# Warm-up products in column strips, and three weight loads in another place, in a fused state-space and feed-forward kernel

## The chip, the core and the metric

The kernel runs on one core of one Trainium2 chip. The metric is the device time of one execution in microseconds (us). A core has five engines with a queue of instructions each: TensorE (PE in the profile, its weight loads PEld), VectorE (DVE), ScalarE (ACT), GpSimd (POOL) and SyncE (SP). They wait for one another through semaphores. Transfers are started by SP, ACT or POOL and are carried out by 16 DMA engines. TensorE writes into PSUM, eight banks of 128 x 512 numbers in float32, which ACT or DVE has to read out before a bank can be used again.

## The reference

`x` is 2048 tokens by 512 features. After a layer norm, `xn`, two branches are computed from it and added to `x`:

```
xn  = layernorm(x)
# branch A, a diagonal complex state-space layer
Bu  = xn @ B_bar.T                       # complex, 512 states
h_t = Lam_bar * h_(t-1) + Bu_t           # along 2048 tokens
yA  = 2 * real(h @ C.T) + xn * Dskip
# branch B, a gated feed-forward layer with 1376 hidden units
yB  = (silu(xn @ w_gate) * (xn @ w_up)) @ w_down
out = x + yA + yB
```

Products take bfloat16 and accumulate in float32; the output is bfloat16.

## The kernel before

The 2048 tokens are cut into four chunks `c` of 512 tokens (four tiles of 128 tokens each). Each chunk goes through the same products on TensorE, all of them written out by hand in one order:

- `bproj_tile(c, part, q)` (L365): B's product, real (`part` 0) and imaginary (`part` 1), for four groups `q` of 128 states. It sums four products over the feature blocks `k` into one PSUM bank, with `BT[:, part, k]` as the weights, and ACT copies the bank to `u16` (L372).
- `gateup_tile(c, fi)` (L511): for each of ten full blocks `fi` of 128 hidden units a gate bank and an up bank, each of four products (L445); ACT applies silu to the one and copies the other (L464, L465), DVE multiplies them in pairs of blocks (L460). The eleventh block has only 96 units. For it `gateup_last(c)` (L500) computes the 96 gate columns together with 32 of the up columns (`w_last`), read out by L506 and L507. The other 64 up columns (`wu_last`) are computed for all four chunks at once in `up_halves` (L484, products in L492, in pairs of 64 columns), much later, within `out_chunk(0)`.
- `out_ffn`, `out_pair` and `out_ssm`: the products with `w_down` and with C.

DVE turns the complex recurrence into real scans (rotations L380 to L394, scans L412). Its work is kept in a list, `backlog`, and `pump` puts pieces of it behind each TensorE tile by costs written in the code, so the order on every engine is fixed when the program is built.

The head (L686 to L726) handles the first chunk. While the first tokens are on their way, TensorE runs dummy products on a constant (`dummy(8, CW)`, eight products of 512 columns, then two of 128, L687 and L688; the product is in L660). Then it transposes the first token tiles by products with an identity (L235), and computes gate and up columns of three blocks tile by tile (`head_mm`, L683). The normalisation is on DVE (L220). The last tile of the chunk, and all tiles of later chunks, are transposed by a transfer instead (`xT_dma`, L249, on SP).

Weights are loaded in groups of hidden blocks, `fgroups` (L89): blocks 0 to 1, 2, 3 to 6 and 7 to 9. Most transfers stand on SP's queue in the order of the code: at the start x's first tiles, the first three weight groups and two of B's transposed loads; then `load_mid()` (L143) with x's second chunk, B's remaining real transposes, its four imaginary transposes (`load_bt(1, k)`, L138), the last gate group, the last up group and `w_last`; then the transposes of chunk 1's tokens; then `load_late()` (L154) with x's second half and `w_down` in two halves (L159); then C's eight transposes (L862). `load_late` also puts the load of `wu_last` on ACT's queue (L155). It is called after chunk 0's B products and ahead of its blocks 7 to 10:

```
    load_late()
    for fi in range(G0, FT):
        gateup_tile(0, fi)
```

after which come C's transposes and `bproj_chunk(1)` (L789, called in L864). An engine's queue is in order: a transfer that ACT starts stands among ACT's copies, and if its issue has to wait, what is behind it waits too. Each transfer that SP or ACT starts uses one of eight completion counters, chosen when the program is built.

Of the kernel before, what the change touches and what calls it, by code (L numbers as in the profile page):

```python
# [23 lines left out]
def kernel(  # L24
# [17 lines left out]
    nc = tc.nc  # L42
    _, L, D = A_x.shape
# [3 lines left out]
    CW = 512  # L47
# [4 lines left out]
    KD = D // 128  # L52
    HK = KD // 2
# [6 lines left out]
    LA, LB = 32, 64  # L60
    FL = (FT - 1) * 128
# [12 lines left out]
    def bank(shape=(128, CW), dtype=F32):  # L74
        return psum.tile(list(shape), dtype, name="ps")
# [6 lines left out]
    wg_v = B_w_gate.rearrange("(k p) f -> p k f", p=128)  # L82
    wu_v = B_w_up.rearrange("(k p) f -> p k f", p=128)
# [6 lines left out]
    wg_g, wu_g = [], []  # L90
# [5 lines left out]
    wu_last = const.tile([128, KD, LB], BF16, name="wu_last")  # L96
# [14 lines left out]
    def load_w1(q, tiles, view, gi):  # L111
        a, b = fgroups[gi]
        q.dma_start(out=tiles[gi][:], in_=view[:, :, a * 128:min(F, b * 128)])
# [23 lines left out]
    def load_bt(part, k):  # L137
        nc.sync.dma_start_transpose(out=BT[:, part, k, :], in_=(A_B_re, A_B_im)[part][:, k * 128:(k + 1) * 128])  # L138
# [4 lines left out]
    def load_mid():  # L143
        nc.sync.dma_start(out=xall[:, TPC:2 * TPC, :], in_=x_v[:, TPC:2 * TPC, :])
        for k in range(HK, KD):
            load_bt(0, k)
        for k in range(KD):
            load_bt(1, k)
        load_w1(nc.sync, wg_g, wg_v, 3)
        load_w1(nc.sync, wu_g, wu_v, 3)  # L150
        nc.sync.dma_start(out=w_last[:, :, 0:LB + LA], in_=wg_v[:, :, FL:F])
        nc.sync.dma_start(out=w_last[:, :, LB + LA:128], in_=wu_v[:, :, FL + LB:F])

    def load_late():  # L154
        nc.scalar.dma_start(out=wu_last[:], in_=wu_v[:, :, FL:FL + LB])  # L155
        nc.sync.dma_start(out=xall[:, 2 * TPC:NT, :], in_=x_v[:, 2 * TPC:NT, :])
        wd_v = B_w_down[0:FL, :].rearrange("(k p) d -> p k d", p=128)
        for a, b in ((0, FT // 2), (FT // 2, FT - 1)):
            nc.sync.dma_start(out=wd_sb[:, a:b, :], in_=wd_v[:, a:b, :])  # L159


    ones = nc.const_aps.tensor(1.0, (128, CW), BF16)
# [348 lines left out]
    def gateup_tile(c, fi):  # L511
        if fi == FT - 1:
            return gateup_last(c)
        psg = bank()
        gu_mm(psg, wg_g, c, fi, 0, CW)
        psu = bank()
        gu_mm(psu, wu_g, c, fi, 0, CW)
        gu_out(c, fi, psg, psu)
# [113 lines left out]
    def pump(us):  # L632

        owed[0] += us
        while backlog and owed[0] >= backlog[0][0] * 0.5:
            step()
        if not backlog:
            owed[0] = 0.0

    def multiply(keep):  # L640

        while len(products) > keep:
            products.pop(0)()
            owed[0] -= 0.65
# [10 lines left out]
    held = [(bank(), bank()) for _ in range(H)]  # L655
    warm = held[0][0]

    def dummy(n, cols):
        for _ in range(n):
            nc.tensor.matmul(warm[:, 0:cols], lhsT=ones[:, 0:128], rhs=ones[:, 0:cols], start=True, stop=True)  # L660
# [23 lines left out]
                                 rhs=xnT[:, k, lo * 128:hi * 128], start=(k == 0), stop=(k == KD - 1))  # L684

    allk = range(KD)  # L686
    dummy(8, CW)  # L687
    dummy(2, 128)  # L688
    ln_stats(0)
    rstd_act(0)  # L690
# [4 lines left out]
    rstd_act(1)  # L695
    xT_pe(0, on_dve=(0,))
    dummy(4, 128)
    norm_dve(1)
    ln_stats(2)
# [20 lines left out]
    norm_dve(3)  # L720
    xT_dma(3)
    load_mid()
    head_mm(0, 2, 3, range(0, HK), range(H))
    head_mm(1, 2, 3, range(0, HK), range(H))
# [55 lines left out]
    for fis in (range(4, EARLY - 1), range(EARLY - 1, EARLY)):  # L780
        ps, n = bank(), len(fis)
# [59 lines left out]
    for part in range(2):  # L841
        for q in range(NQ):
# [10 lines left out]
           ["ln2"] * len(norm2) + ["ln3"] * (len(stats3) + len(norm3)))  # L853
    queue("cf", c_ops())
    load_late()
    for fi in range(G0, FT):
        gateup_tile(0, fi)
        pump(GU)
        multiply(1)
    for part, src in enumerate((A_C_re, A_C_im)):  # L860
        for q in range(NQ):
            nc.sync.dma_start_transpose(out=CT[:, part, q, :], in_=src[:, q * 128:(q + 1) * 128])  # L862
# [50 lines left out]
```

## Time and profile before

| | |
|---|---|
| median of 3 runs | 178.35 us |
| lowest and highest | 178.32 and 178.7 us |
| profiled execution | 178.76 us |
| its span, first to last instruction | 177.0 us |
| TensorE busy | 173.5 us, 98% of the span |
| DVE busy | 153.9 us, 87% |
| ACT busy | 95.3 us, 54% |
| POOL busy | 51.8 us, 29% |
| moved by DMA | 16.36 MB, mean 92 GB/s |

The profile is of one execution. A row of a timeline gives start and length in us from the span's start, then the engine, the line of the kernel, the operation, what it writes and reads, its shape, how many such instructions are merged in the row, and in brackets the idle time ahead of it with what ended it. "SPq" and "ACTq" are the issues of transfers from those queues; a row of the DMA view gives the size and the time from issue to landing. The length of a TensorE product in a row includes its way through the array, so products overlap, and the distance between starts is what a product costs. TensorE's clock is half at the beginning of a run and again some time after the last product.

### The profile page before, as it was taken

Reading aid. Unit: us, or ns where it says so; the run is one execution under the profiler, and the core shown is the slowest. Engines: PE = TensorE matmul, PEld = TensorE weight load, DVE = VectorE, ACT = ScalarE, POOL = GpSimd, SP = SyncE. Lnnn points to the kernel's source line nnn. Section 1 sums busy time; section 2 is a strip of 40 time slices with the busy share of each in tenths; the row PEclk is TensorE's granted clock in tenths of the full one; section 3 lists DMA queues with packets and bytes.
Section 4 is the critical chain, followed back from the end, with each engine's and each line's share of the span. In section 5 each row is a group of like instructions: output and inputs, shape, how many; then the busy total and the mean of one; then the engine's idle time right before and its main releaser. Section 6 shows DMA issues by size and latency. Waiting matters only on the chain.

```text
span 177.0 us, 2607 instructions
## 1 busy us (share of the span) xinstructions
PE 173.5 (98%) x955; PEld 84.1 (48%) x955; DVE 153.9 (87%) x233; ACT 95.3 (54%) x174; POOL 51.8 (29%) x86
## 2 busy tenths in 40 slices
PE   8999999999999999999999999999999999999993
PEld 2977644444444444444444444444444444444443
DVE  3779999999999997999999999999999999971033
ACT  3477898867797679613666661053866610001300
POOL 6050120002300210029997040058476500001410
PEclk9999999999999999999999999999999999999999
DMA  5998497996440014900000020019699200000652
GB/s 169 306 167 204 91 257 80 305 305 129 89 87 6 0 36 82 355 5 17 17 19 17 0 82 11 0 20 129 88 147 189 46 2 0 0 4 0 63 98 76
DMA packets 31292, 16.36 MB, mean 92 GB/s; under 512 B 20208, under 2 KB 31088, under 8 KB 31248
## 3 DMA queue, kind: packets, MB, share of 16 engines
q1 hardware_dynamic: 24704, 11.51, 27.3%
q0 software_dynamic: 5184, 4.07, 15.9%
q10 hardware_dynamic: 1392, 0.62, 1.7%
q8 instruction: 7, 0.11, 0.3%
q14 instruction: 5, 0.04, 0.1%
HBM read 8.33 MB, written 5.24 MB: 77 GB/s over the span
## 4 chain that ended last, share of the span: by engine, by line
PE 98%; DVE 0%; issue 0%
PE ps L445 35%; PE ps L594 16%; PE ps L370 16%; PE ps L556 10%; PE ps L582 10%; PE ps L683 2%; PE ps L660 2%; PE ps L503 2%; PE ps L759 2%; PE ps L545 2%; PE ps L492 1%; PE ps L235 1%; DVE res L599 0%; PE ps L265 0%
## 5 line engine op out<-in xcount | busy, mean ns | idle before, releaser
L445 PE MATMUL ps<-xnT,wg 128*128 128x512 bf16 (+1 forms) x148 | 36.6, 373 | 0.0
L445 PE MATMUL ps<-xnT,wu 128*128 128x512 bf16 (+1 forms) x148 | 36.6, 373 | 0.0
L412 DVE TENSOR_TENSOR_SCAN g<-r_t,car,u 128x512 bf16<-128x512 f32 x24 | 28.8, 1263 | 0.0
L370 PE MATMUL ps<-xnT,BT 128*128 128x512 bf16 x128 | 28.3, 379 | 0.0
L594 PE MATMUL ps<-CF,wt 128*128 128x512 bf16 (+2 forms) x144 | 28.2, 356 | 0.0
L464 ACT ACTIVATE guT<-ps 128x512 bf16<-128x512 f32 (+1 forms) x40 | 23.5, 587 | 6.7 <-PE ps L445 6.0
L465 ACT CAST u<-ps 128x512 bf16<-128x512 f32 (+1 forms) x40 | 23.0, 575 | 6.9 <-PE ps L445 6.6
L607 ACT CAST res<-ps 128x512 bf16<-128x512 f32 x12 | 6.7, 590 | 36.0 <-PE ps L594 26.8
L445 PEld LDWEIGHTS <-wu 128*128 128x128 bf16 x148 | 14.5, 98 | 16.6
L187 POOL DMA_DIRECT2D gu_rows<-ul x36 | 17.6, 499 | 15.8 <-DVE ul L480 15.8
L445 PEld LDWEIGHTS <-wg 128*128 128x128 bf16 x148 | 14.4, 98 | 16.5
L608 POOL DMA_DIRECT2D out_dram<-res x12 | 10.5, 1220 | 37.4 <-ACT res L607 37.2
L372 ACT CAST u<-ps 128x512 bf16<-128x512 f32 x32 | 18.2, 586 | 6.0 <-PE ps L370 5.9
L594 PEld LDWEIGHTS <-wt 128*128 128x128 bf16 x144 | 13.3, 98 | 15.0 <-issue 1.3
L370 PEld LDWEIGHTS <-BT 128*128 128x128 bf16 x128 | 12.5, 98 | 14.8
L212 POOL TENSOR_TENSOR rstd<-ve,neg_half 128x2 f32<-128x2 f32 (+1 forms) x4 | 5.7, 1418 | 44.4 <-DVE ve L211 44.4
L582 PE MATMUL ps<-wd_sb,guT 128*128 128x512 bf16 x80 | 17.6, 379 | 0.0
L556 PE MATMUL ps<-wd_sb,guT 128*128 128x512 bf16 x80 | 17.4, 379 | 0.0
L460 DVE TENSOR_TENSOR guT<-guT,u 128x1024 bf16<-128x1024 bf16 x20 | 13.4, 677 | 0.0
L582 PEld LDWEIGHTS <-guT 128*128 128x128 bf16 x80 | 7.8, 98 | 9.4
L556 PEld LDWEIGHTS <-guT 128*128 128x128 bf16 x80 | 7.8, 98 | 9.4
L203 DVE BATCH_NORM_STATS2 stats<-xall 128x6 f32<-128x512 bf16 x14 | 9.5, 679 | 1.9 <-DMA xall<-in_A_x_dram 1.8
(120 smaller groups left out, 200.8 us busy)
## 6 DMA issues: line engine op xcount, KB each, us to landing
out_dram<-in_A_x_dram SPq DMA_DIRECT2D x1, 1536.0 KB, 6.8
out_dram<-res POOLq DMA_DIRECT2D x12, 128.0 KB, 3.6
out_dram<-xall POOLq DMA_DIRECT2D x3, 512.0 KB, 7.4
wd_sb<-in_B_w_down_dram SPq DMA_DIRECT2D x2, 640.0 KB, 7.7
xall<-in_A_x_dram SPq DMA_DIRECT2D x1, 1024.0 KB, 5.9
gu_rows<-ul POOLq DMA_DIRECT2D x36, 8.0 KB, 1.6
wg<-in_B_w_gate_dram SPq DMA_DIRECT2D x1, 512.0 KB, 5.0
wu<-in_B_w_up_dram SPq DMA_DIRECT2D x1, 512.0 KB, 6.0
```

What stands on the lines that cost most here:

```text
L187: nc.gpsimd.dma_start(out=gu_rows[c][i * RT:(i + 1) * RT, p, :], in_=product[p * RT:(p + 1) * RT, i * 128:(i + 1) * 128])
L370: nc.tensor.matmul(ps[:], lhsT=BT[:, part, k, q * 128:(q + 1) * 128], rhs=xnT[:, k, c * CW:(c + 1) * CW], start=(k == 0), stop=(k == KD - 1))
L372: nc.scalar.copy(out=u_tiles[c][:, part, q, :], in_=ps[:])
L412: V.tensor_tensor_scan(out=g()[:, part, q, :], data0=r_t[:, q:q + 1].to_broadcast([128, CW]), data1=u_tiles[c][:, part, q, :], initial=ini ...
L445: nc.tensor.matmul(ps[:fs, lo:hi], lhsT=wslice(groups, fi, k), rhs=xnT[:, k, c * CW + lo:c * CW + hi], start=(k == 0), stop=(k == KD - 1))
L460: products.append(lambda: V.tensor_tensor(out=g, in0=g, in1=u, op=ALU.mult))
L464: nc.scalar.activation(out=gu_tile(c)[:, fi, 0:hi], in_=psg[:, 0:hi], func=ACT.Silu)
L465: nc.scalar.copy(out=u_tile(c, fi)[:, fi % 2, 0:hi], in_=psu[:, 0:hi])
L556: nc.tensor.matmul(o[:], lhsT=gu_tiles[k][:, fi, i * 128:(i + 1) * 128], rhs=wd_sb[:, fi, :], start=(fi == 0), stop=False)
L582: nc.tensor.matmul(o[:], lhsT=gu_tiles[c][:, fi, i * 128:(i + 1) * 128], rhs=wd_sb[:, fi, lo:hi], start=(fi == 0), stop=False)
L594: nc.tensor.matmul(o, lhsT=w_tiles[c][:, part, q, i * 128:(i + 1) * 128], rhs=CF[:, part, q, lo:hi], start=(fresh and part == 0 and q == 0 ...
L608: nc.gpsimd.dma_start(out=out_v[:, n, :], in_=res[:], accum_op=ALU.add)
```

## The change

Three edits. The first two of the eight 512-column dummy products become eight products with 32 weight columns each, four per set, written to the four 32-partition strips of the same bank. In `load_mid` the last gate group is loaded between B's second and third imaginary transpose, and the last up group behind the fourth; the number of transfers is the same. The load of `wu_last` stays on ACT's queue but moves from `load_late` to behind chunk 0's last gate and up block, which is behind that block's copy L507 and ahead of the copies L372 of `bproj_chunk(1)`.

```diff
-        for k in range(KD):
-            load_bt(1, k)
-        load_w1(nc.sync, wg_g, wg_v, 3)
-        load_w1(nc.sync, wu_g, wu_v, 3)
+        for groups, view, ks in ((wg_g, wg_v, range(0, HK)), (wu_g, wu_v, range(HK, KD))):
+            for k in ks:
+                load_bt(1, k)
+            load_w1(nc.sync, groups, view, 3)
...
     def load_late():
-        nc.scalar.dma_start(out=wu_last[:], in_=wu_v[:, :, FL:FL + LB])
         nc.sync.dma_start(out=xall[:, 2 * TPC:NT, :], in_=x_v[:, 2 * TPC:NT, :])
...
+    def dummy_groups(n):
+        for _ in range(n):
+            for i in range(0, 128, 32):
+                nc.tensor.matmul(warm[i:i + 32], lhsT=ones[:, 0:32], rhs=ones[:], start=True, stop=True)
+
...
-    dummy(8, CW)
+    dummy_groups(2)
+    dummy(6, CW)
     dummy(2, 128)
...
         multiply(1)
+    nc.scalar.dma_start(out=wu_last[:], in_=wu_v[:, :, FL:FL + LB])
     for part, src in enumerate((A_C_re, A_C_im)):
```

## The prediction

> **What bounds the kernel now.** I read the page's busy times and its chain first, then busy time by stretches, then the timelines around each edit. In the rows by stretches the columns are the length, then busy time of PE, weight loads, DVE, ACT and POOL, the granted clock, the DMA share and GB/s.
>
> ```profile
> span 177.0 us, 2607 instructions
> PE 173.5 (98%) x955; PEld 84.1 (48%) x955; DVE 153.9 (87%) x233; ACT 95.3 (54%) x174; POOL 51.8 (29%) x86
> PE 98%; DVE 0%; issue 0%
> ...
> 6.68:38.71 32.03, 32.03 (x245) 19.03 (x242) 29.05 (x70) 26.42 (x55) 4.17 (x5) 1.00 0.95 210
> 31.96 6.91 PE ps L370 x32
> ```
>
> The chain that ended last is TensorE for 98% of the span, and between 6.68 and 38.71 us TensorE has no gap at all. So nothing that only relieves another engine can shorten the run, and any wait put in front of TensorE lengthens it by its full length: there is no slack later in which to make it up. A full product of 512 columns costs 6.91/32 = 0.216 us, a product tile of four 0.864 us. What is left to win lies ahead of 6.68 us, where products take twice as long per column:
>
> ```profile
> 0.78 3.78 PE L660 MATMUL ps<-const-bfloat16-1.0 128*128 128x512 bf16 x10 [0.78 <-PEq L897]
> 4.11 0.41 DVE L220 TENSOR_SCALAR xall<-xall,mv,rstd 128x512 bf16<-128x512 bf16 x1
> 4.25 0.31 PE L660 MATMUL ps<-const-bfloat16-1.0 128*128 128x128 bf16 x1
> 4.58 0.61 PE L235 MATMUL ps<-ident,xall 128*128 128x128 bf16 x4
> 5.37 0.41 DVE L220 TENSOR_SCALAR xall<-xall,mv,rstd 128x512 bf16<-128x512 bf16 x1
> 6.26 0.59 PE L235 MATMUL ps<-ident,xall 128*128 128x128 bf16 x4
> 6.68 0.61 PE L683 MATMUL ps<-xnT,wu 128*128 128x128 bf16 x8
> 7.14 0.38 PE L683 MATMUL ps<-xnT,wg 128*128 128x128 bf16 x4
> ```
>
> The 4352 dummy columns take 3.78 us (0.87 ns each); eight products of 128 columns from 6.68 to 7.14 take 0.46 us (0.45 ns each), those from 6.26 to 6.68 take 0.42 us for four (0.82 ns). The clock turns up at about 6.68 us. The sum below is made against the profiled execution, 178.76 us (span 177.0 plus 1.76 around it); the median of the runs is 178.35, 0.41 lower, so the same difference is laid on the median.
>
> **Part 1, the dummies.** Two products over the full array become eight of 32 columns in four column strips. Nothing in the trace runs four strips; the nearest rows are the pairs of half-width products of L492:
>
> ```profile
> 71.73 0.81 PE L582 MATMUL ps<-wd_sb,guT 128*128 128x512 bf16 x3
> 72.47 1.92 PE L492 MATMUL ps<-xnT,wu_last 128*64 128x512 bf16 x16
> 74.32 0.39 PE L594 MATMUL ps<-CF,wt 128*128 128x512 bf16 x1
> ```
>
> Sixteen half-width products take 1.85 us up to the next full one, against 8 x 0.216 = 1.73: the two strips of a pair run side by side, with 0.12 for leaving the mode; three full products take 0.74 instead of 0.65 ahead of them, 0.09 for entering it. So two sets of four should take about as long as two full products, plus some 0.2 us for leaving at half clock. The dummies' products stop issuing at about 4.36 (the last starts at 4.25 and takes 0.11 at this clock) and the transposes of 4.58 wait for the normalisation that ends at 4.52, so 0.2 of it is covered. Bounds: 0 (they cannot make the transposes start before 4.52) and, if strips ran one after another, 6 x 0.43 = 2.6 us more dummies less the cover, of which about half, 1.2 us, would be left because the rest would then run after the clock has turned. The L492 rows are near the lower end: I take 0.05 us.
>
> **Part 2, SP's order.** The last gate group's load moves ahead of B's last two imaginary transposes.
>
> ```profile
> 18.85 7.07 PE L370 MATMUL ps<-xnT,BT 128*128 128x512 bf16 x32
> 18.62 1.26 SPq L138 DMA_TRANSPOSE BT<-in_A_B_im_dram  x1
> 19.93 0.58 SPq L113 DMA_DIRECT2D wg<-in_B_w_gate_dram  x1
> ...
> BT<-in_A_B_im_dram SPq DMA_TRANSPOSE x1, 2.7
> ```
>
> The last transpose now lands at 18.62 + 2.7 = 21.3. TensorE needs it for the fourth product of the first imaginary tile: B's products start at 18.85 (16 real ones at 0.216, then three more), so at 22.95: 1.6 us of cover. The load ahead of it costs its issue, 0.58, and its transfer, bounded by nothing and about 1.3 us (384 KB at the 300 GB/s of the row 30.70:39.20 below); 0.6 to 1.9 us later, so a wait of 0 to 0.3 us. I take 0; what there is would be swallowed by part 3, whose end does not depend on it. The gate group lands earlier, but TensorE does not wait for it now: gain 0.
>
> **Part 3, the last up columns.** The load of wu_last leaves ACT's queue at 25.97 and comes back behind the last copy of chunk 0's gate and up work (L507). Taking it out is a gain for the transfers:
>
> ```profile
> 23.14 1.22 SPq L249 DMA_TRANSPOSE xnT<-xall  x1
> 25.76 2.48 SPq L249 DMA_TRANSPOSE xnT<-xall  x1
> 28.32 1.29 SPq L249 DMA_TRANSPOSE xnT<-xall  x1
> 30.91 0.68 SPq L159 DMA_DIRECT2D wd_sb<-in_B_w_down_dram  x1
> 25.97 0.41 ACTq L155 DMA_DIRECT2D wu_last<-in_B_w_up_dram  x1
> wd_sb<-in_B_w_down_dram SPq DMA_DIRECT2D x1, 640.0 KB, 8.3
> ...
> 30.70:39.20 8.50, 8.50 (x41) 3.88 (x40) 8.36 (x15) 6.79 (x13) 0.00 (x0) 1.00 1.05 300
> ```
>
> The one slow transpose issue (2.48 against 1.2 to 1.3) is the one beside wu_last's transfer. Without it everything behind on SP goes out 1.26 us earlier, and as the transfers are saturated from 30.7 to 39.2, the second half of wd_sb, now landing at 30.91 + 8.3 = 39.2, lands at about 37.9.
>
> Putting it back is the cost. Each transfer of SP and ACT gets one of eight completion counters, and its issue waits until the counter's earlier transfer has landed. In the built program wu_last's issue used to wait for w_last's first part, which had landed; in its new place the counter's earlier transfer is **the second half of wd_sb**. ACT is in order, so it stands there from 33.2 (end of L507) to 37.9:
>
> ```profile
> 31.80 7.07 PE L370 MATMUL ps<-xnT,BT 128*128 128x512 bf16 x32
> 32.61 0.58 ACT L507 CAST ul<-ps 32x512 bf16<-32x512 f32 x1
> 33.21 1.11 ACT L372 CAST u<-ps 128x512 bf16<-128x512 f32 x2
> 24.32 2.23 ACT L372 CAST u<-ps 128x512 bf16<-128x512 f32 x4
> 43.23 0.58 ACT L465 CAST u<-ps 128x512 bf16<-128x512 f32 x1 [0.27 <-PE ps L445]
> 49.90 0.66 DVE L460 TENSOR_TENSOR guT<-guT,u 128x1024 bf16<-128x1024 bf16 x1
> ```
>
> Behind the wait stand the eight copies L372 of B's chunk 1, which free TensorE's PSUM banks. By the built program's waits the sixth product tile of that chunk needs the bank that the first copy frees. That tile starts at 31.80 + 5 x 0.864 = **36.12**. In the changed kernel it starts after 37.9 + 0.41 (the issue) + 0.56 (one copy, 2.23/4) + about 0.1 for two semaphores = **39.0**. TensorE stands **2.9 us**. After that ACT needs 0.56 per copy against TensorE's 0.864, so it does not stop again. VectorE goes on: its next product that needs ACT's late work is at 49.90, some 6 us behind the copy that it reads (L465 at 43.23), so it hides the shift. wu_last itself is needed at 72.47 only.
>
> Bounds of the 2.9: if the slow transpose issue stays slow for another reason, wd_sb lands at 39.2 and TensorE stands 4.2; if the transfers gain half a microsecond more, 2.4.
>
> **Sum:** 0.05 + 0 + 2.9 = +2.9 us, 181.7 against the profiled run, 181.3 against the median.
>
> **The rivals.**
>
> Clock earlier. If four strips counted as more activity, the clock could turn before 4.58. The two tile transposes could then not move before 5.78 (the normalisation of 5.37 ends), 0.48 before 6.26, and run in 0.23 instead of 0.42 us: about 0.6 us gained, on TensorE and, through the same chain, on SP. The stall stays: +2.3, 180.7. For it: the turn comes 5.9 us after the first product. Against: two strips of half width take the time of one full product, no sign that they are more work. The Trainium skill ("TensorE: Matmul & The Clock Gate", the part on what is actually happening) says that a free-running window of about 3.4 us has to be busy before the clock opens. By that rule a window only partly filled at the start has failed here, and a fuller first one would bring this case. 18%.
>
> Transfers no earlier: +4.2, 182.5. For it: the changed order puts a load between transposes, which may slow them elsewhere. 14%.
>
> The clock falls in the stall.
>
> ```profile
> 173.81 0.44 PE L594 MATMUL ps<-CF,wt 128*128 128x128 bf16 x5
> ...
> 177.30:179.00 1.70, 0.00 (x0) 0.00 (x0) 0.00 (x0) 0.00 (x0) 0.00 (x0) 0.51 0.01 5
> ```
>
> After the last product (over at 174.25) the granted clock is halved by 177.3, 3 us later; a stall of 2.9 is just short of that. If it fell, some 3.4 us of products would run at half speed, 1.7 us more: 183.0. The Trainium skill (same page, the part on why this matters) warns of idle gaps above about 3 us. By that rule the stall is at the edge. 7%.
>
> Strips one after another: the +1.2 of part 1 on top, 182.5. Against it stands L492. 2%.
>
> Not slower: ACT's wait ends before TensorE needs the bank. It decides at 36.12 - 1.07 = 35.05 us: if wd_sb's second half lands by then the stall is nothing, and 178.3 (177.7 with the earlier clock) is left. That needs a landing 4.1 us earlier, where the earlier issue accounts for 1.3 and the transfer stretch runs at its full rate. It would also hold if ACT's issue did not really hold ACT. 4%.
>
> **How the numbers follow.** Forecast 181.3 with 55%, own range 180.8 to 181.9. Range 180.4 to 182.8: it takes in the earlier clock, the later landing and the serial strips, and leaves out the fallen clock and the case without a stall. A measurement of this kernel can tell about 0.2%, 0.36 us. Slower 0.95; within 0.03 and faster 0.02, both from the last rival.
>
> **What would show it.** In the changed profile TensorE's B products of chunk 1 (L369 there) break off after the fifth tile, for 2.9 us, until about 39; ACT has no instruction between 33.2 and its issue of wu_last at about 37.9, right after wd_sb lands; the third transpose issue is back to 1.2 us; the columns ahead of 6.68 still cost twice those behind. I am wrong if ACT's copies go on at 33.2, if the sixth tile starts at 36.1, or if the first 6.7 us shrink by more than a microsecond.

## The result, and the profile after

| | before | after |
|---|---|---|
| median of 6 runs each | 178.33 us (178.23 to 178.7) | 180.22 us (179.44 to 180.7) |
| ratio, 95% interval | | 1.0097 [1.0068, 1.0126] |
| profiled execution | 178.76 us | 180.09 us |
| its span | 177.0 us | 178.3 us |

The change costs 1.9 us on the medians and 1.33 us between the two profiled executions. It is slower, as forecast, but by less than forecast (+2.9), and below the range. First the page of the changed kernel: span, busy times, and the chain that ended last.

```profile
span 178.3 us, 2619 instructions
...
PE 173.5 (97%) x961; PEld 83.8 (47%) x961; DVE 153.9 (86%) x233; ACT 94.3 (53%) x174; POOL 51.9 (29%) x86
...
PE 80%; DVE 10%; DMA 5%; SPq 1%; issue 1%; POOL 1%; ACT 0%; ACTq 0%; DVEq 0%; POOLq 0%
```

TensorE is busy for exactly as long as before, 173.5 us, in a span that is 1.3 us longer: it has no more work, it stands. And the chain is no longer TensorE alone (98% before). At one place it leaves TensorE and follows a DMA for 5% of the span (the page names wd_sb), and from there runs back through the engines that had fed that transfer. The waits of TensorE and of ScalarE say where; the numbers are the total in us, the number of times and the longest:

```profile
PE ps L502 <- ACT u L371: 1.2, 1, 1.2
...
ACT u L371 <- DMA wd_sb<-in_B_w_down_dram: 6.3, 1, 6.3
```

The timeline around it:

```profile
31.70 7.07 PE L369 MATMUL ps<-xnT,BT 128*128 128x512 bf16 x32
32.51 0.58 ACT L506 CAST ul<-ps 32x512 bf16<-32x512 f32 x1
38.93 0.41 ACTq L865 DMA_DIRECT2D wu_last<-in_B_w_up_dram  x1
39.38 4.01 ACT L371 CAST u<-ps 128x512 bf16<-128x512 f32 x8 [6.30 <-DMA wd_sb<-in_B_w_down_dram]
40.02 1.02 PE L502 MATMUL ps<-xnT,w_last 128*128 128x512 bf16 x4 [1.25 <-ACT u L371]
```

Read it from the ACTq row. ScalarE ends its last copy at 33.09 and does nothing until wu_last's issue goes out at 38.93. That is when the second half of w_down lands (issued at 30.24, 8.7 us to landing, rows further down). The trace records the completion counter of each issue, eight different ones in all: wu_last and the second half of w_down have the same one. Only behind the issue, 6.3 us after the last copy, come the eight copies of B's chunk 1. TensorE meanwhile has run all 32 products of that chunk without a break (31.70, one row). It stands only at the next tile, L502, the ninth in a row since ScalarE stopped freeing banks. In the kernel before the same tile follows without a gap:

```profile
38.71 1.03 PE L503 MATMUL ps<-xnT,w_last 128*128 128x512 bf16 x4
```

40.02 less 38.71 is 1.31 us, which is the difference of the profiled executions (1.33). By stretches (length, busy time of PE, weight loads, DVE, ACT and POOL, granted clock, DMA share, GB/s):

```profile
31.70:38.62 6.92, 6.92 (x33) 3.14 (x32) 6.85 (x8) 1.38 (x3) 0.00 (x0) 1.00 1.18 316
38.62:40.02 1.40, 0.15 (x1) 0.00 (x0) 1.40 (x2) 0.64 (x2) 0.00 (x0) 1.00 1.20 246
40.02:72.00 31.98, 31.98 (x149) 14.50 (x149) 29.81 (x51) 29.28 (x53) 4.37 (x3) 1.00 0.34 75
```

One gap, with full work on TensorE on both sides. ScalarE is idle in the first row for 5.5 of 6.9 us, and VectorE goes on throughout. TensorE's clock does not fall in the gap: the tile behind it costs 0.86 us (40.02 to 40.88), as before. The column of the granted clock alone would not show that in this trace, which holds no record of the clock; the column reads 1.00 for the first 6 us too, where products take twice as long.

### The profile page after: what moved, and what is told of

It is laid out like the page before. It is cut to its first block, busy times and chain, and to the rows that moved or that the text cites. A ratio compares the mean times of both kernels' runs of the same rounds, so it can differ in the third digit from the quotient of the medians.

```text
span 178.3 us, 2619 instructions
## 1 busy us (share of the span) xinstructions
PE 173.5 (97%) x961; PEld 83.8 (47%) x961; DVE 153.9 (86%) x233; ACT 94.3 (53%) x174; POOL 51.9 (29%) x86
## 4 chain that ended last, share of the span: by engine, by line
PE 80%; DVE 10%; DMA 5%; SPq 1%; issue 1%; POOL 1%; ACT 0%; ACTq 0%; DVEq 0%; POOLq 0%
PE ps L444 29%; PE ps L593 16%; PE ps L555 10%; PE ps L581 10%; PE ps L369 8%; DMA wd_sb<-in_B_w_down_dram 5%; DVE pm L304 2%; PE ps L664 2%; PE ps L544 2%; PE ps L502 2%; DVE pm L303 2%; PE ps L687 2%; DVE stats L202 1%; PE ps L491 1%; DVE guT L459 1%; DVE pm L295 1%
## 5 line engine op out<-in xcount | busy, mean ns | idle before, releaser
L444 PE MATMUL ps<-xnT,wg 128*128 128x512 bf16 (+1 forms) x148 | 36.6, 373 | 0.0
L444 PE MATMUL ps<-xnT,wu 128*128 128x512 bf16 (+1 forms) x148 | 36.6, 373 | 0.0
L371 ACT CAST u<-ps 128x512 bf16<-128x512 f32 x32 | 17.7, 598 | 10.6 <-DMA wd_sb<-in_B_w_down_dram 6.3
L444 PEld LDWEIGHTS <-wu 128*128 128x128 bf16 x148 | 14.5, 98 | 16.6
L444 PEld LDWEIGHTS <-wg 128*128 128x128 bf16 x148 | 14.4, 98 | 16.5
```

Of the source, the lines that this page charges most:

```text
L371: nc.scalar.copy(out=u_tiles[c][:, part, q, :], in_=ps[:])
L444: nc.tensor.matmul(ps[:fs, lo:hi], lhsT=wslice(groups, fi, k), rhs=xnT[:, k, c * CW + lo:c * CW + hi], start=(k == 0), stop=(k == KD - 1))
```

## The experiments

Each edit is a diff against the changed kernel unless the text says that it is against the kernel before. Each line of results gives the median, lowest and highest, and the ratio to the kernel before, run on the same chip.

**Parts 1 and 2 without the move.**

```diff
     def load_late():
+        nc.scalar.dma_start(out=wu_last[:], in_=wu_v[:, :, FL:FL + LB])
...
-    nc.scalar.dma_start(out=wu_last[:], in_=wu_v[:, :, FL:FL + LB])
```

> The changed kernel with the load of wu_last back in load_late, so the strips and SP's new order alone. If the whole loss is ACT's wait for wd_sb (my theory), there is no gap of TensorE at 38 us and the time is that of before, 178.3 us within 0.3. If the strips or SP's order cost something of their own, as the rival has it, the time stays near the changed kernel's 180.2.

Measured: 178.3 us (178.15 to 178.95, 11 runs), 0.9994 [0.9984, 1.0004], and no gap on TensorE. The strips and the new order together are worth nothing that can be told.

**The move alone**, the same two lines the other way, in the kernel before.

> The kernel before with the load of wu_last moved and nothing else. By my theory the wait for the second half of wd_sb is there all the same: wd_sb lands at 39.2 in the profile before, less what the missing transfer beside the token transposes gives, so ACT's first copy ends at 39.9 to 40.2 and TensorE stands 1.2 to 1.5 us in front of the gate columns of the last block: 179.5 to 180.7. By the rival (strips or order) it is 178.3. By the prediction's reading of the banks (the sixth product tile needs the first copy) it would be 181.3 or more.

Measured: 179.93 us (179.64 to 180.54, 6 runs), 1.0081 [1.0064, 1.0098]. The same stall at the same tile, from the same transfer:

```profile
38.96 0.42 ACTq L859 DMA_DIRECT2D wu_last<-in_B_w_up_dram  x1
39.42 2.05 ACT L371 CAST u<-ps 128x512 bf16<-128x512 f32 x4 [6.36 <-DMA wd_sb<-in_B_w_down_dram]
40.05 1.02 PE L502 MATMUL ps<-xnT,w_last 128*128 128x512 bf16 x4 [1.30 <-ACT u L371]
```

The loss belongs to the move alone.

**wu_last issued two product tiles later**, to learn how far TensorE runs ahead of ScalarE's copies.

```diff
                 bproj_tile(c, part, q)
+                if c == 1 and part == 0 and q == 1:
+                    nc.scalar.dma_start(out=wu_last[:], in_=wu_v[:, :, FL:FL + LB])
...
-    nc.scalar.dma_start(out=wu_last[:], in_=wu_v[:, :, FL:FL + LB])
```

> The changed kernel with the issue of wu_last two copies later, behind the second tile of B's chunk 1. ACT then waits for the first of C's transposes, which lands at about 39.4, and holds the third copy instead of the first. If TensorE runs out of banks eight tiles after the held copy, it needs the third bank at 38.61 + 1.73 = 40.3 and gets it at 39.4 + 0.41 + 0.56 + 0.1 = 40.5: a stand of 0 to 0.4 us, 178.3 to 178.8. By the prediction's reading (five tiles after it) it needs that bank at 37.8 and stands 2.7 us: 181.

Measured: 178.8 us (178.16 to 179.18, 12 runs), 1.0012 [0.9998, 1.0027]. Two copies now go ahead of the wait, the third behind it, and TensorE's stall moves on by exactly two tiles, from L502 to the up tile of L444:

```profile
33.13 1.10 ACT L371 CAST u<-ps 128x512 bf16<-128x512 f32 x2
38.63 1.03 PE L502 MATMUL ps<-xnT,w_last 128*128 128x512 bf16 x4
39.50 1.03 PE L444 MATMUL ps<-xnT,wg 128*128 128x512 bf16 x4
39.72 0.45 ACTq L800 DMA_DIRECT2D wu_last<-in_B_w_up_dram  x1
40.21 2.05 ACT L371 CAST u<-ps 128x512 bf16<-128x512 f32 x4 [5.97 <-DMA CT<-in_A_C_re_dram]
40.85 1.02 PE L444 MATMUL ps<-xnT,wu 128*128 128x512 bf16 x4 [0.32 <-ACT u L371]
```

First copy held, ninth tile late; third copy held, eleventh tile late: a copy frees the bank of the tile eight places on. ScalarE waits 6 us here too, and TensorE loses only 0.49 us in this trace (40.85 less 39.50 + 0.864); on the medians so small a loss is not clear of the noise. The counter's earlier transfer is now one of C's transposes, which the row names.

**ScalarE released early by another counter.** One load of 512 KB that nothing needs, ahead of w_down on SyncE, shifts the counters by one; wu_last then shares its counter with x's second half.

```diff
         nc.sync.dma_start(out=xall[:, 2 * TPC:NT, :], in_=x_v[:, 2 * TPC:NT, :])
+        nc.sync.dma_start(out=CF[:, 0, :, :], in_=wg_v[:, :, 0:512])
```

> The changed kernel with one more load of 512 KB put into SP's queue between x's second half and wd_sb (into a tile that is written over later; it is not needed). It shifts the completion counters by one: wu_last, at the same place on ACT, now waits for x's second half, which lands at 35.3, not for wd_sb. By my theory ACT's first copy is done at 36.4, ahead of the 38.6 at which TensorE needs its bank, and the time is 178.3 within 0.4, although more is loaded and wd_sb lands later. If the place on ACT, the transfers' load or wd_sb itself were what costs, it would be as slow as the changed kernel or slower, 180.2 to 182.

Measured: 179.08 us (179.0 to 179.49, 5 runs), 1.0037 [1.0024, 1.0049]. wu_last's issue goes out when x's second half has landed (issued at 29.05, 5.7 us to landing). TensorE's gap is gone, though the extra load makes w_down land later (40.1 us); but 0.7 us stay, more than the 0.4 that was allowed for:

```profile
34.76 0.39 ACTq L866 DMA_DIRECT2D wu_last<-in_B_w_up_dram  x1
38.25 1.03 PE L503 MATMUL ps<-xnT,w_last 128*128 128x512 bf16 x4
...
173.84 0.29 DVE L599 TENSOR_TENSOR res<-ps,part_end 128x128 bf16<-128x128 f32 x1 [0.15 <-PE ps L594]
```

From VectorE's last addition (173.84) to the end of the span (177.2) are 3.4 us. In the kernel before they are 2.7 (174.29 to 177.0), in the changed kernel too (175.60 to 178.3). What is lost here is lost behind all the work. Two further runs take that apart.

**The same without shifting the counters of the end:** w_down in one transfer, and the spare load behind it, so that the number of transfers stays.

```diff
-        for a, b in ((0, FT // 2), (FT // 2, FT - 1)):
-            nc.sync.dma_start(out=wd_sb[:, a:b, :], in_=wd_v[:, a:b, :])
+        nc.sync.dma_start(out=wd_sb[:], in_=wd_v)
+        nc.sync.dma_start(out=CF[:, 0, :, :], in_=wg_v[:, :, 0:512])
```

> The changed kernel, with wu_last's load at its place on ScalarE, but w_down comes in one transfer instead of two and a transfer of 512 KB that nothing needs stands behind it on SyncE. The number of transfers stays, so the counters at the end of the run are dealt as in the changed kernel; the earlier user of wu_last's counter is now the last transpose of chunk 1's tokens, landed near 30.5. Theory (ScalarE's hold behind w_down is the whole loss): ScalarE goes on at 33.2, TensorE has no gap, 178.3 (ratio 1.000). Rival (something else about the load at this place costs, for instance its transfer beside C's transposes): 179 or more, without ScalarE's wait. Rival (the 0.67 us that the other extra load cost is the load's own weight): 179.0; by the theory that it comes from the order in which the counters are looked at in the end, 178.3.

Measured: 178.52 us (178.2 to 178.88, 11 runs), 1.0005 [0.9996, 1.0014].

```profile
31.75 0.39 ACTq L865 DMA_DIRECT2D wu_last<-in_B_w_up_dram  x1
32.95 1.10 ACT L371 CAST u<-ps 128x512 bf16<-128x512 f32 x2
```

The load stands at the changed kernel's place in the program, on the counter of the last transpose of chunk 1's tokens, which landed before, and ScalarE does not wait: the loss is gone. It is the wait that costs, not the load's place or its bytes.

**Only the extra load, in the kernel before.**

```diff
         nc.sync.dma_start(out=xall[:, 2 * TPC:NT, :], in_=x_v[:, 2 * TPC:NT, :])
+        nc.sync.dma_start(out=CF[:, 0, :, :], in_=wg_v[:, :, 0:512])
```

> The kernel before, with nothing but the extra transfer of 512 KB that nothing needs between x's second half and w_down: the counters of all later transfers shift by one, so the last store falls on the first of the eight counters instead of the last. Theory (the rest of the earlier run with this load is a matter of the end, where SyncE looks at the eight counters one after another): TensorE's last product ends where it did (about 174.2), the time is up by 0.5 to 0.7 us, to 178.9 to 179.1, all of it behind the last store's landing. Rival (the load itself disturbs the transfers): TensorE ends later, or the end of the run looks as before and the time is 178.4.

Measured: 179.17 us (178.82 to 179.37, 5 runs), 1.0037 [1.0023, 1.0051], by the median a little more than expected. The work ends as before (VectorE's last addition and the last store 0.09 us earlier):

```profile
174.20 0.29 DVE L600 TENSOR_TENSOR res<-ps,part_end 128x128 bf16<-128x128 f32 x1 [0.15 <-PE ps L595]
174.52 0.35 SPq L603 DMA_DIRECT2D out_dram<-res  x1
...
L909 SPq EVENT_SEMAPHORE  x8: 28/28/28, 176.0 to 176.5; - x8
...
L909 SPq DRAIN  x3: 7/13/120, 176.6 to 177.3; - x3
```

The third row is from the view of the line behind the kernel's end, cut to 175.95 to 176.5 us: SyncE's looks at the counters, with their number, shortest, median and longest time in ns, and the first and last start; the fourth is from the same view of the whole run. The last store lands at 176.0 (174.52 and 1.5), and eight looks follow, one after another, until 176.5. In the kernel before, the same view from 176.04 on:

```profile
L908 SPq DRAIN  x3: 7/7/7, 176.2 to 176.5; - x3
L908 SPq EVENT_SEMAPHORE  x2: 17/22/28, 176.1 to 176.4; - x2
```

There the last store lands at 176.1, one look at 176.1 ends it, and the closing drains begin at 176.2; the other counters had been looked at while the store was on its way. The traces record the last store's counter: the highest number of the eight (118) in the kernel before, in the changed kernel and in the run before this one, the lowest (101) in the two kernels with one transfer more. That they are looked at in a fixed order, the lowest first, is inferred from this and from the number of looks behind the landing. Seven further looks at 0.07 us are 0.5 of the 0.7 us; SyncE's last drain, 0.12 us long instead of 0.007, makes up part of the rest, and why it is longer stays open.

**wu_last issued by GpSimd at the same place.**

```diff
-    nc.scalar.dma_start(out=wu_last[:], in_=wu_v[:, :, FL:FL + LB])
+    nc.gpsimd.dma_start(out=wu_last[:], in_=wu_v[:, :, FL:FL + LB])
```

> The changed kernel with wu_last's load issued by GpSimd at the same place of the program instead of by ScalarE. ScalarE isn't held, and one transfer fewer uses the eight counters. Theory: no gap on TensorE, 178.3 to 178.5 (ratio 1.000 to 1.001). Rival (the load's transfer or its issue costs whatever engine starts it): 179 or more.

Measured: 178.42 us (178.26 to 178.76, 11 runs), 1.0002 [0.9993, 1.0011]; no gap on TensorE. The same load at the same place is free from a queue that nobody waits for.

**The changed kernel once more.**

> The changed kernel once more, for a second trace. Theory (TensorE's wait ends 1.07 us after the second half of w_down has landed, so the run's time moves with that landing): the span is the landing plus 139.4 us; with the landing between 38.3 and 39.5, 179.4 to 180.7. Rival (the spread of the changed kernel's runs has another source): the span does not follow the landing within 0.2 us.

Measured: 179.88 us (179.24 to 180.07, 4 runs), 1.0076 [1.0058, 1.0094]; profiled execution 180.07, span 178.3. The landing was the same in both traces, so the expected dependence was not tried; but another one shows:

```profile
31.49 7.07 PE L369 MATMUL ps<-xnT,BT 128*128 128x512 bf16 x32
40.02 0.59 PE L502 MATMUL ps<-xnT,w_last 128*128 128x512 bf16 x2 [1.46 <-ACT u L371]
```

TensorE came 0.21 us earlier than in the first trace (31.70), waited 0.21 us longer (1.46 against 1.25), and went on at the same 40.02.

**The strips alone**, in the kernel before (`dummy_groups(2)` and `dummy(6, CW)` in place of `dummy(8, CW)`).

> The kernel before with nothing but the strips: its first two dummy products of 512 columns become eight in four column strips. Theory (the strips are covered by the wait for the normalisation, and the moment at which products reach their full rate differs from run to run whatever the dummies): 178.35, ratio 1.000 within 0.001. Rival (strips make the clock turn earlier; in the seven traces with strips products reached the full rate between about 4.2 and 6.4 us, in the three without between 6.3 and 6.7): 0.1 to 0.5 us faster, ratio 0.997 to 0.9994.

Measured: 178.51 us (178.22 to 178.85, 12 runs), 1.0004 [0.9996, 1.0013]. In this trace the products reach their full rate at the first transposes (four in 0.41 us, where the kernel before takes 0.61), yet the runs are not faster than those of the kernel before.

```profile
4.58 0.41 PE L235 MATMUL ps<-ident,xall 128*128 128x128 bf16 x4
...
31.26 7.07 PE L370 MATMUL ps<-xnT,BT 128*128 128x512 bf16 x32
```

**SyncE's order alone**, in the kernel before (the first hunk of the diff).

> The kernel before with nothing but the new order of SyncE's loads (the last gate group between B's imaginary transposes, the last up group behind them). Theory (nobody waits for these loads before or after): no gap on TensorE in its B products of chunk 0, 178.35, ratio 1.000 within 0.001. Rival (the order costs or gains something that the strips had offset in the earlier run of both together): 0.2 us or more to either side.

Measured: 178.3 us (178.2 to 178.82, 12 runs), 0.9996 [0.9987, 1.0004]; no gap in B's products of chunk 0.

**All eight dummies in strips**, with the new order and without the move (`dummy_groups(8)`).

> The changed kernel without the move of wu_last, and with all eight 512-column dummy products in strips instead of two. Theory (strips neither cost nor gain behind the wait for the normalisation): the dummies end no later than before by more than 0.3 us, 178.3 to 178.5. Rival (strips make the clock turn earlier): with four times as many, products reach the full rate by about 5 us or sooner, 0.3 to 0.6 us faster, ratio 0.9966 to 0.998. Second rival (strips run one after another when there are many): dummies up to 9 us longer, and the run longer by several us.

Measured: 179.26 us (178.68 to 179.59, 7 runs), 1.0041 [1.0026, 1.0056]: a miss for each of the three. The dummies end where they did, the full rate comes at about 6.5 us, and the loss sits elsewhere, at B's imaginary transposes:

```profile
22.95 0.10 PEld L370 LDWEIGHTS <-BT 128*128 128x128 bf16 x1 [0.52 <-DMA BT<-in_A_B_im_dram]
23.42 1.62 PEld L370 LDWEIGHTS <-BT 128*128 128x128 bf16 x9 [0.38 <-DMA BT<-in_A_B_im_dram]
```

Two weight loads wait for the third and fourth transpose; the products lose 0.46 us by the distances between their starts, about half of the 0.87 by which the medians differ.

**The same with the old order.** This is the kernel before with `dummy_groups(8)` in place of `dummy(8, CW)`.

> All eight 512-column dummy products in strips, with SyncE's loads in the order of the kernel before and wu_last at its old place. It tells apart why the earlier kernel with all strips lost 0.4%, of which its trace shows 0.45 us on TensorE waiting for B's imaginary transposes. Theory (the loss is the new order's: a load that stands ahead of B's last two transposes uses up their margin, and a wait follows where a run's transfers are late): without the new order no wait on TensorE near 22.5 us, 178.3 to 178.6 (ratio 1.000 to 1.001). Rival (the loss is the strips': the clock turns later or something in the head is longer): 178.9 to 179.4 (ratio 1.003 to 1.006), with products reaching their full rate later than 6.7 us or the transposes of 4.6 us starting later.

Measured: 178.61 us (178.2 to 178.84, 12 runs), 1.0005 [0.9993, 1.0016], no wait of TensorE near 22.5 us.

```profile
0.78 3.60 PE L661 MATMUL ps<-const-bfloat16-1.0 128*32 128x512 bf16 x32 [0.78 <-PEq L902]
4.32 0.39 PE L665 MATMUL ps<-const-bfloat16-1.0 128*128 128x128 bf16 x2
4.59 0.61 PE L235 MATMUL ps<-ident,xall 128*128 128x128 bf16 x4
6.27 0.53 PE L235 MATMUL ps<-ident,xall 128*128 128x128 bf16 x4
```

Thirty-two strip products take at most 0.2 us longer than eight full ones (the two short ones behind them start at 4.32, where the kernel before's second starts at 4.25), and the full rate comes no earlier than in the kernel before. With the old order the last transpose landed at 22.55 us in this trace (issue 19.10), 1.2 us later than the 21.3 of the kernel before, and TensorE, which needs it at about 22.95, did not wait. With the new order and the same strips it landed at 23.4. So the new order's load ahead of it does use up margin, and here it was enough to make TensorE wait; in the run of the order alone the last transpose landed at 22.7, and TensorE did not wait. Why the transposes are later with all eight dummies in strips, also with the old order, stays open.

## Why the prediction was half right

**Right: what stands, why, and that the rest is free.** The bound was TensorE without a gap, and a wait put in front of it came through in full. The load's issue held ScalarE behind the second half of w_down, from 33.1 to 38.93; the copies L371 stood behind it; VectorE did not feel it (the product forecast at 49.90 started at 49.83); ScalarE did not hold TensorE again. The move alone gives the loss and its absence takes the loss away. Part 1 (0.05 us) and the 0 of part 2 agree with the runs of each alone: 1.0004 [0.9996, 1.0013] and 0.9996 [0.9987, 1.0004].

**Wrong: which tile needs the bank.** The step that failed is "the sixth product tile of that chunk needs the bank that the first copy frees". It is the ninth: with eight banks in turn, a bank comes round eight tiles later. The run with the load two tiles later shows the same distance. I had counted every ScalarE instruction as one on the counter that TensorE's products wait for, while some raise it by two; that this is where the reading of the built program went wrong is not tested by a run. With the right tile, TensorE needs the copy at 31.80 + 8 x 0.864 = 38.71 instead of 36.12. This takes 2.59 us off the stall.

**Wrong: "everything behind on SP goes out 1.26 us earlier".** The changed kernel's queue of SyncE, and the DMA row of the second half of w_down:

```profile
23.05 5.90 SPq L248 DMA_TRANSPOSE xnT<-xall  x4
30.24 0.52 SPq L158 DMA_DIRECT2D wd_sb<-in_B_w_down_dram  x1
wd_sb<-in_B_w_down_dram SPq DMA_DIRECT2D x1, 640.0 KB, 8.7
```

The four transposes take 5.90 us of issue against 6.47 before (23.14 to 28.32 + 1.29): the third is back to 1.22, as forecast, but now the second takes 1.97, though wu_last's transfer is no longer beside it. In the run of the move alone one of the four is slow too (1.76), and in the last run above, with wu_last at its old place beside them, none is (four in 5.15). So my reason for the slow issue was wrong; what makes one slow stays open. The half went out 0.67 us earlier (30.24 against 30.91) and landed only some 0.25 us earlier (38.9 against 39.2), because it took 8.7 us instead of 8.3: in a stretch in which the transfers are saturated, an earlier issue mostly waits longer. The other traces say the same: in the nine without a spare load and with at most two sets of strips, this half was issued anywhere from 29.78 to 30.91 and landed between 38.7 and 39.2 (in the two with eight sets it landed at 37.8). The wait's end came at 40.02 instead of 39.0. This adds 1.02 us. The rival "transfers no earlier" had this part nearly right, but not its reason, the changed order: in the run of the move alone, with the old order, the half landed at 38.9 as well.

**Wrong: "the same difference is laid on the median".** A stall that ends with a transfer has a fixed end, not a fixed length. The second trace of the changed kernel shows it (0.21 earlier, 0.21 longer). Without a stall the run's time follows the start of B's chunk 1: 31.24, 31.26, 31.33, 31.54, 31.80 and 31.84 us in six traces (GpSimd's issue, strips alone, no move, spare load behind w_down, before, order alone) went with 178.26, 178.25, 178.30, 178.52, 178.76 and 178.82, the start plus 146.96 to 147.02 each time. The two traces with one more transfer lie 0.67 us above that line, which is the end of the run told above. That start varies with the moment at which the products reach their full rate; in the traces with no stall ahead of it, it was 31.24 to 31.35 where that came before about 5.5 us, 31.49 to 31.54 at about 6.0, and 31.68 to 31.84 at 6.3 to 6.7. The kernel before's profiled run was a late one (31.80), its median run about 0.4 earlier (178.35 less 147.0 is 31.35). The changed kernel throws such an early start away, since it waits for w_down anyway. The difference of the medians, 1.89, is larger than that of the profiled runs, 1.33, by 0.56: 0.43 because the kernel before's median (178.33) lies below its profiled run, 0.13 because the changed kernel's lies above its own. That the median run starts early is worked out, not traced, and why the changed kernel's runs spread from 179.24 to 180.70 is not shown.

The sum of the steps: 2.9 - 2.59 + 1.02 + 0.56 = 1.9 us. The first three give the 1.33 of the profiled runs; the last is what is left to the medians. Two of the errors hid each other. With the right tile alone I would have said +0.3 (39.0 less 38.71), a change that can hardly be measured; with the right landing alone, +3.9. That the forecast of a slower kernel held is in part luck.

**The rivals.** A clock that falls in the stall: no, the tiles behind it come at full rate, 0.86 us apart, and the stall is only 1.3 us. Strips one after another: no, 32 of them take 3.60 us. Clock earlier: not by the strips, since neither two nor eight sets made the runs faster (1.0004 and 1.0005); the moment differs from run to run whatever the dummies are. The traces alone would have misled: it came between about 4.2 and 6.4 us in the eight with two sets, and between 6.3 and 6.7 in the six with none or eight. But the traced execution of the order alone, without strips, was the slowest of its twelve (178.82), and seven of the other eleven took 178.20 to 178.31, which by the sum above needs a start as early as 31.2 to 31.3. That clock would also have gained nothing in the changed kernel, for the reason above; the prediction priced it as if it did. Not slower: its condition was the right kind, with the wrong number. With the ninth tile the landing has to be by 38.71 - 1.07 = 37.6 us, not 35.05, which is 1.3 us from what happened and not 4.

## What to carry to other kernels

An engine's wait for a counter holds everything behind it on that engine, so before a load is moved on a compute engine's queue, find which earlier transfer its counter belongs to and when that lands. The cost is then (landing + issue + copy) less the moment at which the consumer runs out of buffers, and that moment is as many tiles on as there are buffers (eight banks here): check the count in the trace, by the tile that reuses the bank. Where the end of a wait is set by a transfer, compare ends and not lengths: anything that makes the waiting engine arrive earlier is lost in it.

## What was not expected of the hardware

- One more transfer that nothing needs cost 0.7 us at the end of the run in two kernels (1.0037 in both), with TensorE's work unchanged: the completion counters are looked at one after another, about 0.07 us each, and the last store's counter then came first instead of last.
- The moment at which products reach their full rate differed between about 4.2 us (the run without the move) and 6.7 us among traces whose first product always started at 0.78 or 0.79. By the traces above, this is most of the 0.6 us by which runs of one kernel without a stall differ. In the twelve traces that record the granted clock, full speed lasts 170.67 or 174.08 us whatever the kernel did. The two differ by 3.41 and are 50 and 51 times 3.413 us, so the clock seems to come and go in fixed steps of that length. The Trainium skill ("TensorE: Matmul & The Clock Gate", the part on what is actually happening) says that the window is free-running, so that the number of slow products changes from run to run; the traces agree, by the moments and the steps just given.
- A transfer's issue waits on the engine that issues it, 5.8 us here (33.09 to 38.93). The Trainium skill ("DMA: Bandwidth & Descriptors", the part on the anatomy of one DMA) says that DMA engines do not wait on semaphores and that the wait happens on the issuing sequencer; the trace agrees, and shows what stands behind it.
